# Block products of the pair stages gathered onto each other's PSUM banks, with ScalarE copying out in between

## The chip, the core and the metric

The kernel runs on one core of one Trainium2 chip. The metric is the device time of one launch in microseconds; the median of three runs is given. A core has five engines with a queue each: TensorE (PE in the rows, its weight loads PEld), VectorE (DVE), ScalarE (ACT), GpSimd (POOL) and SyncE (SP, which issues the DMAs). Each engine works its queue off in order and waits on semaphores for the others.

## The reference

Three stages follow each other: attention with a band mask, a mixture of four experts, and a gated network.

```python
scores = scale * np.matmul(q, k.transpose(0, 1, 3, 2)) + bias      # 2 x 8 heads, 768 positions, 64 wide
a = softmax(np.where(keep, scores, -1e9));  attn = a @ v           # keep: 8 global keys or 96 local ones
p = domain_probs / (domain_probs.sum(-1, keepdims=True) + 1e-09)   # x: 1536 tokens x 512
for e in range(4):
    out += p[:, e:e+1] * (np.maximum(x @ w1[e], 0.0) @ w2[e])      # 512 -> 1024 -> 512
h = (x @ w1) * (x @ w2)                                            # 512 -> 1024, twice
return (h @ w3) @ w_out                                            # 1024 -> 1024 -> 512
```

All of it is in float32. The last two weights are multiplied with each other first (w34 = w3 @ w_out).

## The kernel before

Every float32 operand of the large products is split into a high and a low half: `split` (L49, L50) casts the high half on ScalarE and subtracts it from the source on VectorE or GpSimd. The helper `three` (L55 to L57) then runs three matmuls of 128 x 128 by 128 x 512: high by high, high by low, low by high. Tokens stand in three chunks of 512 columns, 0 to 2.

Engines are written in program order (`manual_schedule`): what the code issues first on an engine runs first there.

**The pair stages.** For part of the work two chunks of tokens (1 and 2) and two row blocks of weights are taken together as a 2 by 2 block product, which needs seven block products in place of eight, on sums and differences of blocks. The blocks of the weights are a11, a12, a22 and the sums s1 to s4, those of the tokens b11 to b22 and the differences t1 to t4. One block product is `product(a, b)`: six matmuls onto one PSUM bank (`z`, four banks in turn). From the seven products the four results are added up:

c11 = a11 b11 + a12 b21; with u2 = a11 b11 + s2 t2, c12 = u2 + s1 t1 + s4 b22; with u3 = u2 + s3 t3, c22 = u3 + s1 t1 and c21 = u3 + a22 t4.

There are two such stages:

- The expert pair stage has eight steps (0 to 7): steps 0 to 3 for expert 3, steps 4 to 7 for expert 2, each for two of the eight hidden rows of that expert. `Pairs.run` does a step. Between the products it calls `issue(j)` (the down products onto the banks `o` that are due, twelve matmuls each; after the last of a row, four multiplications by the gate share on VectorE, L749, and four additions on GpSimd, L750), `prep(0)` (casts of the next step's weights a11, a12, a22), `prep(1)` (their four sums, L642, on VectorE, then casts and low halves on ScalarE and GpSimd) and, in steps 4 to 7, `prep(2)` (casts and low halves of two down weights of the second expert, on ScalarE and VectorE). `out` ends a result: ReLU to the high half on ScalarE (L541), low half on VectorE (L542).
- The gate pair stage has eight steps too. `Gate.run` does one: the same products; two of the four results are multiplied by the other two (L1124, L1128) and split. `issue(n)` there is three matmuls of the final product of the step before. `sums_of_w` (L1066) and the casts prepare the next step's weights.

Before, each of the seven products of a step goes to a bank of its own. ScalarE copies the first (L661, L1101), and VectorE adds the other six in seven additions (L649, L1097), two of them from s1's bank.

Of the kernel before, what the change touches and what calls it, by code (L numbers as in the profile page):

```python
# [8 lines left out]
F32 = mybir.dt.float32  # L9
# [4 lines left out]
ALU = mybir.AluOpType  # L14
# [4 lines left out]
P = 128  # L19
# [8 lines left out]
CW = 512  # L28
# [9 lines left out]
LAG = 2  # L38
# [14 lines left out]
def three(nc, out, wh, wl, xh, xl, start, stop):  # L53

    nc.tensor.matmul(out, wh, xh, start=start, stop=False)  # L55
    nc.tensor.matmul(out, wh, xl, start=False, stop=False)  # L56
    nc.tensor.matmul(out, wl, xh, start=False, stop=stop)  # L57
# [524 lines left out]
class Pairs:  # L582


# [62 lines left out]
    def run(self, n, issue, prep, out):  # L647
        nc, tmp = self.nc, self.tmp
        add = lambda o, a, b: nc.vector.tensor_tensor(o, a, b, op=ALU.add)  # L649

        def product(a, b):
            z = self.ps_z.tile([P, CW], F32, name="z")
            h, l = self.at(n, ("a11", "a12", "a22", "s1", "s2", "s3", "s4").index(a))
            xh, xl = self.x_operand(b)
            for k in range(2):
                ks = slice(k * P, (k + 1) * P)
                three(nc, z, h[:, ks], l[:, ks], xh[:, k], xl[:, k], k == 0, k == 1)
            return z

        s1, s6 = tmp(), tmp()  # L660
        nc.scalar.copy(s1, product("a11", "b11"))  # L661
        add(s6, s1, product("s2", "t2"))
        prep(0)
        issue(0)
        add(s1, s1, product("a12", "b21"))
        out(0, 1, s1)
        u3 = tmp()
        add(u3, s6, product("s3", "t3"))
        prep(1)
        issue(1)  # L670
        z = product("s1", "t1")
        c22 = tmp()
        add(c22, u3, z)
        add(s6, s6, z)
        out(1, 2, c22)
        prep(2)
        issue(2)
        add(u3, u3, product("a22", "t4"))
        out(1, 1, u3)
        issue(3)  # L680
        add(s6, s6, product("s4", "b22"))
        out(0, 2, s6)


def experts_and_gate(tc, g, x_hi, x_lo, slots, experts, first_time):

    nc = tc.nc
    name = "" if first_time else "g"
    with ExitStack() as ctx:
# [142 lines left out]
        for n in range(last + 1):  # L832
            i, gr = divmod(n, FC // 2)
            e = pairs[i]
            if gr:
                downs = [[(e, 1, 2 * gr - 2)], [], [(e, 1, 2 * gr - 1)], []]
            elif i:
                downs = ends(pairs[i - 1])
            else:
                downs = [work[-LAG:], [], [], []]  # L840
# [125 lines left out]
class Gate:  # L966
# [111 lines left out]
    def run(self, f, between):  # L1078
# [3 lines left out]

        def product(a, b):
            z = self.ps_z.tile([P, CW], F32, name="z")
            h, l = blocks[a]
            xh, xl = self.x_operand(b)
            for k in range(2):
                ks = slice(k * P, (k + 1) * P)
                three(nc, z, h[:, ks], l[:, ks], xh[:, k], xl[:, k], k == 0, k == 1)
            return z  # L1090

        def issue(n):
            if between[n]:
                between[n]()

        more = bool(self.fetched)
        add = lambda out, a, b: nc.vector.tensor_tensor(out, a, b, op=ALU.add)  # L1097
        part = (lambda n: self.sums_of_w(n)) if more else (lambda n: None)
        s1 = self.pool.tile([P, CW], F32, name="prob")
        s6, u3, c22, c11 = self.tmp  # L1100
        nc.scalar.copy(s1, product("a11", "b11"))  # L1101
        add(s6, s1, product("s2", "t2"))
        if more:
            self.split_w()
        issue(0)
        add(c11, s1, product("a12", "b21"))
        part(0)
        part(1)
        add(u3, s6, product("s3", "t3"))
# [5 lines left out]
        z = product("s1", "t1")  # L1115
        add(c22, u3, z)
        h2 = self.pool.tile([P, CW], F32, name="t", bufs=3)
        add(h2, s6, z)
        issue(2)
        z = product("a22", "t4")  # L1120
        hh, hl = self.place()
        h1 = self.pool.tile([P, CW], F32, name="t", bufs=3)
        add(h1, u3, z)
        nc.vector.tensor_tensor(h1, h1, c11, op=ALU.mult)  # L1124
        split(nc, hh, hl, h1)
        issue(3)
        add(h2, h2, product("s4", "b22"))
# [124 lines left out]
```

## Time and profile before

| | |
|---|---|
| median of three runs | 835.33 us (835.03 to 836.26) |
| span of the profiled execution (the time the profile gives for it) | 833.3 us |
| TensorE busy | 821.4 us, 4006 matmuls |
| VectorE, ScalarE, GpSimd busy | 518.4, 288.4, 310.1 us |
| expert pair stage, its eight steps | 427.4 to about 570 us |
| gate pair stage | 703.7 to 801.7 us |

The span runs from the first to the last instruction of the program in the trace; the device time of a run also holds what lies around it. Matmuls are pipelined: a matmul of 512 columns is shown with 0.39 us, though the next starts sooner, so starts are compared here, not durations. In a row of a timeline stand the start, the duration, the engine, the line, the operation, output and inputs, the shape and the count of merged operations; square brackets give the idle time ahead and what ended it.

### The profile page before, as it was taken

To read this page: it belongs to the slowest core of one execution; us is meant where nothing else is said; L and a number is where in the kernel's file an instruction comes from. 1 tells how busy PE (TensorE), PEld (TensorE's weight loads), DVE (VectorE), ACT (ScalarE), POOL (GpSimd) and SP (SyncE) were. 2 spreads that over 40 slices of the span, in tenths; PEclk is the share of its full clock that TensorE was granted. 3 is DMA by queue.
4 is the path that set the end of the run, shared out by engine and by line. 5 is a ranking of instruction groups with operands and counts; after the bars stand their busy time and mean duration, and the time that the engine had idled before them with its cause. 6 is when DMAs were issued, how large, how long until landed. Compare 5 with 4: busy or idle time off the path is not lost.

```text
span 833.3 us, 11131 instructions
## 1 busy us (share of the span) xinstructions
PE 821.4 (99%) x4006; PEld 668.4 (80%) x4006; DVE 518.4 (62%) x962; ACT 288.4 (35%) x609; POOL 310.1 (37%) x318
## 2 busy tenths in 40 slices
PE   8999999999999999999999999999999999999996
PEld 4777888888888888888888888888788888888875
DVE  7998355557755556787738563665633743887840
ACT  6998221223321213333314321332443332333210
POOL 3687013534356564560344341422380003333300
PEclk9999999999999999999999999999999999999999
DMA  6762233547553456643101101020522210201011
GB/s 217 228 202 78 77 115 113 160 154 232 175 165 113 160 170 192 214 162 114 63 26 52 39 25 64 35 81 25 190 99 86 93 53 26 101 26 52 1 51 55
DMA packets 38709, 89.22 MB, mean 107 GB/s; under 512 B 3896, under 2 KB 10344, under 8 KB 38644
## 3 DMA queue, kind: packets, MB, share of 16 engines
q1 hardware_dynamic: 38644, 88.41, 32.7%
q8 instruction: 34, 0.56, 0.3%
q14 instruction: 31, 0.25, 0.1%
HBM read 74.74 MB, written 13.66 MB: 106 GB/s over the span
## 4 chain that ended last, share of the span: by engine, by line
PE 89%; POOL 3%; ACT 3%; DVE 2%; issue 1%; DMA 0%; SPq 0%; POOLq 0%; ACTq 0%; DVEq 0%
PE z L55 18%; PE z L57 18%; PE z L56 18%; PE o L57 11%; PE o L55 11%; PE o L56 11%; POOL pt L308 2%; ACT pt L269 2%; POOL sl L50 1%; DVE t L262 1%; ACT ptT L294 0%; DMA words<-in_n_local_dram 0%; PE sp L55 0%; PE sp L56 0%; PE sp L57 0%
## 5 line engine op out<-in xcount | busy, mean ns | idle before, releaser
L57 PE MATMUL z<-xh,sl 128*128 128x512 f32 x428 | 166.5, 389 | 0.0
L55 PE MATMUL z<-xh,sh 128*128 128x512 f32 x428 | 166.5, 389 | 0.0
L56 PE MATMUL z<-xl,sh 128*128 128x512 f32 x428 | 166.5, 389 | 0.0
L498 POOL TENSOR_TENSOR cr<-cr,cb 128x512 f32<-128x512 f32 x40 | 51.6, 1289 | 125.3 <-issue 118.8
L50 POOL TENSOR_TENSOR sl<-wr,sh 128x256 fp32r<-128x256 f32 (+1 forms) x44 | 40.8, 943 | 150.0 <-ACT sh L49 149.7
L57 PEld LDWEIGHTS z<-xh,sl 128*128 128x128 f32 x428 | 80.4, 188 | 17.2 <-DVE sl L50 0.2
L55 PEld LDWEIGHTS z<-xh,sh 128*128 128x128 f32 x428 | 80.4, 188 | 16.5
L56 PEld LDWEIGHTS z<-xl,sh 128*128 128x128 f32 x428 | 80.3, 188 | 16.6
L50 DVE TENSOR_TENSOR sl<-wr,sh 128x1024 fp32r<-128x1024 f32 (+1 forms) x57 | 70.7, 1245 | 23.1 <-ACT sh L49 22.4
L49 ACT CAST sh<-wr 128x1024 fp32r<-128x1024 f32 (+2 forms) x101 | 75.4, 766 | 21.3 <-PE z L56 10.3
L750 POOL TENSOR_TENSOR acc<-acc,t 128x512 f32<-128x512 f32 x36 | 49.3, 1404 | 84.8 <-DVE t L749 84.8
L483 POOL TENSOR_SCALAR ca<-ca 128x512 f32<-128x512 f32 x40 | 61.5, 1537 | 36.8 <-DMA raw<-in_w_out_dram 36.8
L649 DVE TENSOR_TENSOR t<-t,z 128x512 f32<-128x512 f32 x56 | 37.4, 680 | 32.0 <-PE z L57 27.7
L55 PE MATMUL z<-sh,sh 128*128 128x512 f32 x128 | 49.9, 390 | 0.8 <-DVE t L749 0.8
L56 PE MATMUL z<-sl,sh 128*128 128x512 f32 x128 | 49.8, 389 | 0.0
L57 PE MATMUL z<-sh,sl 128*128 128x512 f32 x128 | 49.8, 389 | 0.0
L269 ACT ACTIVATE pt<-t,negmax 128x256 f32<-128x256 f32 (+1 forms) x96 | 45.9, 479 | 8.9 <-DVE negmax L262 7.7
L308 POOL TENSOR_TENSOR pt<-pt,r 128x256 f32<-128x256 f32 (+1 forms) x72 | 40.8, 595 | 15.3 <-DVE r L237 12.6
L262 DVE CUSTOM_DVE_ANT_0 t<-sp,bias 128x256 f32<-128x256 f32 (+1 forms) x96 | 34.6, 393 | 1.8 <-ACT bias L224 0.4
L50 POOL TENSOR_TENSOR sl<-t,sh 128x256 fp32r<-128x256 f32 (+1 forms) x24 | 23.0, 973 | 31.3 <-ACT sh L49 31.0
L55 PE MATMUL o<-h0h,sh 128*128 128x512 f32 x84 | 32.8, 390 | 0.0
L57 PE MATMUL o<-h0h,sl 128*128 128x512 f32 x84 | 32.7, 389 | 0.0
(254 smaller groups left out, 1738.9 us busy)
## 6 DMA issues: line engine op xcount, KB each, us to landing
wr<-in_w_moe_dram SPq DMA_DIRECT2D x44, 512.0 KB, 4.4
raw<-in_w3t_dram SPq DMA_DIRECT2D x16, 512.0 KB, 4.3
raw<-in_w_ab_dram SPq DMA_DIRECT2D x16, 512.0 KB, 4.6
wr<-wab_d SPq DMA_DIRECT2D x16, 512.0 KB, 3.3
raw<-in_w_out_dram SPq DMA_DIRECT2D x8, 512.0 KB, 5.0
w3t_d<-cr SPq DMA_DIRECT2D x16, 256.0 KB, 2.5
wab_d<-cr SPq DMA_DIRECT2D x16, 256.0 KB, 2.4
wr<-w3t_d SPq DMA_DIRECT2D x8, 512.0 KB, 3.3
```

Source lines behind the costliest of these rows:

```text
L49: nc.scalar.copy(hi, src)
L50: (lo_engine or nc.vector).tensor_tensor(lo, src, hi.bitcast(F32), op=ALU.subtract)
L55: nc.tensor.matmul(out, wh, xh, start=start, stop=False)
L56: nc.tensor.matmul(out, wh, xl, start=False, stop=False)
L57: nc.tensor.matmul(out, wl, xh, start=False, stop=stop)
L262: nc.vector.tensor_tensor_reduce(out=t[:, 0:w], in0=sp[hh % 2][:, hh // 2, 0:w], in1=bb, scale=-SCALE, scalar=3.0e38, op0=ALU.add, op1=ALU ...
L269: nc.scalar.activation(pt[:, hh, 0:w], t[:, 0:w], AF.Exp, bias=g.negmax[:, u * H + h : u * H + h + 1], scale=-1.0, accum_out=sums[:, h : h ...
L308: nc.gpsimd.tensor_tensor(pt[:, hh, 0:w], pt[:, hh, 0:w], r[:, hh : hh + 1].to_broadcast([P, w]), op=ALU.mult)
L483: nc.gpsimd.tensor_scalar(a, a, 2.0**-15, None, op0=ALU.max)
L498: nc.gpsimd.tensor_tensor(rest, rest, top.bitcast(F32), op=ALU.add)
L649: add = lambda o, a, b: nc.vector.tensor_tensor(o, a, b, op=ALU.add)
L750: nc.gpsimd.tensor_tensor(acc[c][:, d], acc[c][:, d], t, op=ALU.add)
```

## The change

The products of a step that belong to one sum are added up in PSUM: `product(a, b, onto)` runs its six matmuls onto a bank that holds an earlier product. Two banks are used so: `first` holds a11 b11, then also s2 t2 (u2), then s3 t3 (u3), then a22 t4 (c21); `both` holds s1 t1 and then also s4 b22. Between, ScalarE copies what is needed on its own: p1 = a11 b11, u2 and u3. VectorE keeps three additions: c11 = p1 + a12's bank, c22 = u3 + `both`, c12 = u2 + `both`. c21 is read from `first` itself. The products are issued in the order a11, a12, s2, s1, s3, a22, s4. In the expert stage the downs of steps 0 to 3 and 5 to 7 are issued after s2 and after s3, `prep(1)` after c22's `out`, and `prep(2)` after a22's `out`. `skip_group_check` is a flag of the program's builder.

```diff
--- before.py
+++ after.py
@@ -50,11 +50,11 @@
     (lo_engine or nc.vector).tensor_tensor(lo, src, hi.bitcast(F32), op=ALU.subtract)
 
 
-def three(nc, out, wh, wl, xh, xl, start, stop):
-
-    nc.tensor.matmul(out, wh, xh, start=start, stop=False)
-    nc.tensor.matmul(out, wh, xl, start=False, stop=False)
-    nc.tensor.matmul(out, wl, xh, start=False, stop=stop)
+def three(nc, out, wh, wl, xh, xl, start, stop, more=False):
+
+    nc.tensor.matmul(out, wh, xh, start=start, stop=False, skip_group_check=more)
+    nc.tensor.matmul(out, wh, xl, start=False, stop=False, skip_group_check=more)
+    nc.tensor.matmul(out, wl, xh, start=False, stop=stop, skip_group_check=more)
 
 
 def iota_f32(nc, pool, width, base, step, name):
@@ -581,6 +581,7 @@
 
 class Pairs:
 
+    BLOCKS = ("a11", "a12", "a22", "s1", "s2", "s3", "s4")
 
 
     def __init__(self, nc, pool, tmp, ps_z, experts):
@@ -646,40 +647,57 @@
 
     def run(self, n, issue, prep, out):
         nc, tmp = self.nc, self.tmp
-        add = lambda o, a, b: nc.vector.tensor_tensor(o, a, b, op=ALU.add)
-
-        def product(a, b):
-            z = self.ps_z.tile([P, CW], F32, name="z")
-            h, l = self.at(n, ("a11", "a12", "a22", "s1", "s2", "s3", "s4").index(a))
-            xh, xl = self.x_operand(b)
-            for k in range(2):
-                ks = slice(k * P, (k + 1) * P)
-                three(nc, z, h[:, ks], l[:, ks], xh[:, k], xl[:, k], k == 0, k == 1)
-            return z
-
-        s1, s6 = tmp(), tmp()
-        nc.scalar.copy(s1, product("a11", "b11"))
-        add(s6, s1, product("s2", "t2"))
+        product = Products(nc, self.ps_z, self.x_operand, lambda a: self.at(n, self.BLOCKS.index(a)))
+
+        first = product("a11", "b11")
+        p1 = product.copy(first, tmp())
+        z = product("a12", "b21")
+        c11 = product.plus(z, p1, tmp())
+        product("s2", "t2", first)
+        u2 = product.copy(first, tmp())
         prep(0)
         issue(0)
-        add(s1, s1, product("a12", "b21"))
-        out(0, 1, s1)
-        u3 = tmp()
-        add(u3, s6, product("s3", "t3"))
+        out(0, 1, c11)
+        both = product("s1", "t1")
+        product("s3", "t3", first)
+        u3 = product.copy(first, tmp())
+        issue(1)
+        c22 = product.plus(both, u3, tmp())
+        out(1, 2, c22)
         prep(1)
-        issue(1)
-        z = product("s1", "t1")
-        c22 = tmp()
-        add(c22, u3, z)
-        add(s6, s6, z)
-        out(1, 2, c22)
+        product("a22", "t4", first)
+        out(1, 1, first)
         prep(2)
         issue(2)
-        add(u3, u3, product("a22", "t4"))
-        out(1, 1, u3)
+        product("s4", "b22", both)
+        out(0, 2, product.plus(both, u2, tmp()))
         issue(3)
-        add(s6, s6, product("s4", "b22"))
-        out(0, 2, s6)
+
+
+class Products:
+
+
+    def __init__(self, nc, ps_z, x_operand, w_operand):
+        self.nc, self.ps_z, self.x, self.w = nc, ps_z, x_operand, w_operand
+
+    def __call__(self, a, b, onto=None):
+
+        more = onto is not None
+        z = onto if more else self.ps_z.tile([P, CW], F32, name="z")
+        h, l = self.w(a)
+        xh, xl = self.x(b)
+        for k in range(2):
+            ks = slice(k * P, (k + 1) * P)
+            three(self.nc, z, h[:, ks], l[:, ks], xh[:, k], xl[:, k], k == 0 and not more, k == 1, more)
+        return z
+
+    def copy(self, z, to):
+        self.nc.scalar.copy(to, z)
+        return to
+
+    def plus(self, z, more, to):
+        self.nc.vector.tensor_tensor(to, more, z, op=ALU.add)
+        return to
 
 
 def experts_and_gate(tc, g, x_hi, x_lo, slots, experts, first_time):
@@ -833,11 +851,11 @@
             i, gr = divmod(n, FC // 2)
             e = pairs[i]
             if gr:
-                downs = [[(e, 1, 2 * gr - 2)], [], [(e, 1, 2 * gr - 1)], []]
+                downs = [[(e, 1, 2 * gr - 2)], [(e, 1, 2 * gr - 1)], [], []]
             elif i:
                 downs = ends(pairs[i - 1])
             else:
-                downs = [work[-LAG:], [], [], []]
+                downs = [[w] for w in work[-LAG:]] + [[], []]
 
             def issue(j):
                 for e, c, f in downs[j]:
@@ -1079,52 +1097,44 @@
 
         nc = self.nc
         blocks = self.made.pop(0)
-
-        def product(a, b):
-            z = self.ps_z.tile([P, CW], F32, name="z")
-            h, l = blocks[a]
-            xh, xl = self.x_operand(b)
-            for k in range(2):
-                ks = slice(k * P, (k + 1) * P)
-                three(nc, z, h[:, ks], l[:, ks], xh[:, k], xl[:, k], k == 0, k == 1)
-            return z
+        product = Products(nc, self.ps_z, self.x_operand, blocks.__getitem__)
 
         def issue(n):
             if between[n]:
                 between[n]()
 
         more = bool(self.fetched)
-        add = lambda out, a, b: nc.vector.tensor_tensor(out, a, b, op=ALU.add)
         part = (lambda n: self.sums_of_w(n)) if more else (lambda n: None)
-        s1 = self.pool.tile([P, CW], F32, name="prob")
-        s6, u3, c22, c11 = self.tmp
-        nc.scalar.copy(s1, product("a11", "b11"))
-        add(s6, s1, product("s2", "t2"))
+        u2, u3, c22, c11 = self.tmp
+        first = product("a11", "b11")
+        p1 = product.copy(first, self.pool.tile([P, CW], F32, name="prob"))
+        z = product("a12", "b21")
+        product.plus(z, p1, c11)
+        product("s2", "t2", first)
+        product.copy(first, u2)
         if more:
             self.split_w()
-        issue(0)
-        add(c11, s1, product("a12", "b21"))
         part(0)
         part(1)
-        add(u3, s6, product("s3", "t3"))
+        both = product("s1", "t1")
+        issue(0)
+        product("s3", "t3", first)
+        product.copy(first, u3)
         part(2)
         part(3)
         if more:
             self.split_s()
         issue(1)
-        z = product("s1", "t1")
-        add(c22, u3, z)
-        h2 = self.pool.tile([P, CW], F32, name="t", bufs=3)
-        add(h2, s6, z)
         issue(2)
-        z = product("a22", "t4")
+        product.plus(both, u3, c22)
+        product("a22", "t4", first)
         hh, hl = self.place()
         h1 = self.pool.tile([P, CW], F32, name="t", bufs=3)
-        add(h1, u3, z)
-        nc.vector.tensor_tensor(h1, h1, c11, op=ALU.mult)
+        nc.vector.tensor_tensor(h1, c11, first, op=ALU.mult)
         split(nc, hh, hl, h1)
         issue(3)
-        add(h2, h2, product("s4", "b22"))
+        product("s4", "b22", both)
+        h2 = product.plus(both, u2, self.pool.tile([P, CW], F32, name="t", bufs=3))
         nc.vector.tensor_tensor(h2, h2, c22, op=ALU.mult)
         split(nc, *self.waiting[f], h2)
         return hh, hl
```

The next rows are VectorE's in step 0 of the expert pair stage, before the change: L749 the multiplications after a down, L649 the additions, L542 low halves, L642 the sums of weights.

```order
L649 TENSOR_TENSOR t<-t,z 128x512
L749 TENSOR_TENSOR t<-o_4047,prob 128x512
L749 TENSOR_TENSOR t<-o_4048,prob 128x512
L749 TENSOR_TENSOR t<-o_4049,prob 128x512
L749 TENSOR_TENSOR t<-o_4050,prob 128x512
L649 TENSOR_TENSOR t<-t,z 128x512
L542 SCALAR_TENSOR_TENSOR h0l<-t,h0h 128x512
L649 TENSOR_TENSOR t<-t,z 128x512
L642 TENSOR_TENSOR t<-wr 128x256
L642 TENSOR_TENSOR t<-t,wr 128x256
L642 TENSOR_TENSOR t<-wr 128x256
L642 TENSOR_TENSOR t<-wr,t 128x256
```

And the same place after the change (the additions are now L699, the multiplications L767, the sums L643).

```order
L699 TENSOR_TENSOR t<-t,z 128x512
L542 SCALAR_TENSOR_TENSOR h0l<-t,h0h 128x512
L767 TENSOR_TENSOR t<-o_4047,prob 128x512
L767 TENSOR_TENSOR t<-o_4048,prob 128x512
L767 TENSOR_TENSOR t<-o_4049,prob 128x512
L767 TENSOR_TENSOR t<-o_4050,prob 128x512
L699 TENSOR_TENSOR t<-t,z 128x512
L542 SCALAR_TENSOR_TENSOR xl_74<-t,xh_71 128x512
L643 TENSOR_TENSOR t<-wr 128x256
L643 TENSOR_TENSOR t<-t,wr 128x256
L643 TENSOR_TENSOR t<-wr 128x256
L643 TENSOR_TENSOR t<-wr,t 128x256
```

The four multiplications stood behind the first of the step's additions and stand now behind c11's low half and ahead of c22's addition, with the weight sums behind that; seven additions have become three.

Next ScalarE around the end of step 5, before the change: L49 casts, of weights (`wr`) and of their sums (`t`), L541 the ReLUs, L661 the copy of the next step's first product.

```order
L49 CAST sh_83<-t 128x256
L541 ACTIVATE xh_71<-t 128x512
L49 CAST sh_81<-wr 128x512
L49 CAST sh_83<-wr 128x512
L541 ACTIVATE h1h<-t 128x512
L541 ACTIVATE xh_71<-t 128x512
L661 COPY t<-z 128x512
```

And after it (the copies are L695).

```order
L49 CAST sh_83<-t 128x256
L541 ACTIVATE h1h<-z 128x512
L49 CAST sh_81<-wr 128x512
L49 CAST sh_83<-wr 128x512
L541 ACTIVATE xh_71<-t 128x512
L695 COPY t<-z 128x512 x2
```

The ReLU of c21 now reads the bank (`z`); it and the copy after c12's ReLU have the casts of the sums and of the down weights ahead of them, as the copy had before.

Last TensorE at the start of a step of the gate pair stage, before the change, with what each waits for: six matmuls of a11 (`xh_72,sh_1560`; the last three stand here) and the first of s2 (`sh_83,sh_1562`).

```order
L55 MATMUL z<-xh_72,sh_1560 128x512
L56 MATMUL z<-xl_75,sh_1560 128x512
L57 MATMUL z<-xh_72,sl_1561 128x512
L55 MATMUL z<-sh_83,sh_1562 128x512 [waits DVE_49,Activation_49]
L56 MATMUL z<-sl_84,sh_1562 128x512
L57 MATMUL z<-sh_83,sl_1563 128x512 [waits Pool_49]
L55 MATMUL z<-sh_83,sh_1562 128x512
```

And after it.

```order
L55 MATMUL z<-xh_72,sh_1560 128x512
L56 MATMUL z<-xl_75,sh_1560 128x512
L57 MATMUL z<-xh_72,sl_1561 128x512
L55 MATMUL z<-xh_72,sh_1560 128x512
L56 MATMUL z<-xl_75,sh_1560 128x512
L57 MATMUL z<-xh_72,sl_1561 128x512
L55 MATMUL z<-xh_72,sh_1560 128x512
L56 MATMUL z<-xl_75,sh_1560 128x512
L57 MATMUL z<-xh_72,sl_1561 128x512
L55 MATMUL z<-sh_83,sh_1562 128x512 [waits Activation_49]
```

a12's six matmuls stand between now, and s2's first matmul, which goes onto a11's bank, waits for ScalarE alone.

## Rows read from the trace of the kernel before

**Rows 1.** The page, part 1: busy us, share of the span, instructions.
```profile
PE 821.4 (99%) x4006; PEld 668.4 (80%) x4006; DVE 518.4 (62%) x962; ACT 288.4 (35%) x609; POOL 310.1 (37%) x318
```

**Rows 2.** Table of stretches: length, busy of each engine, granted clock, DMA.
```profile
427.40:570.00 142.60, 142.32 (x628) 117.58 (x627) 87.49 (x134) 43.48 (x82) 49.25 (x47) 1.00 0.14 46
703.70:801.70 98.00, 98.00 (x433) 80.92 (x431) 75.70 (x114) 28.66 (x53) 34.11 (x30) 1.00 0.12 38
```

**Rows 3.** Timeline of TensorE at the end of step 0: start, duration, operation.
```profile
443.51 0.39 PE L57 MATMUL z<-xh,sl 128*128 128x512 f32 x1
444.17 0.47 PE L55 MATMUL z<-t2h,sh 128*128 128x512 f32 x1 [0.28 <-ACT xh L541]
444.48 0.39 PE L56 MATMUL z<-t2l,sh 128*128 128x512 f32 x1
```

**Rows 4.** Timeline of TensorE at the end of the gate pair stage.
```profile
799.39 0.39 PE L57 MATMUL z<-sh,sl 128*128 128x512 f32 x1
...
801.43 0.39 PE L57 MATMUL z<-xh,sl 128*128 128x512 f32 x1
801.93 0.50 PE L55 MATMUL o<-w34h,h2h 128*128 128x512 f32 x1
802.27 0.39 PE L56 MATMUL o<-w34l,h2h 128*128 128x512 f32 x1
...
803.00 0.40 PE L55 MATMUL o<-w34h,h2h 128*128 128x512 f32 x1
```

**Rows 5.** Timeline of VectorE there.
```profile
799.81 0.69 DVE L1097 TENSOR_TENSOR t<-acc,z 128x512 f32<-128x512 f32 x1 [0.76 <-PE z L57]
800.53 0.69 DVE L1124 TENSOR_TENSOR t<-t,acc 128x512 f32<-128x512 f32 x1
801.91 0.69 DVE L50 TENSOR_TENSOR h2l<-t,h2h 128x512 fp32r<-128x512 f32 x1 [0.69 <-ACT h2h L49]
```

**Rows 6.** Timeline of ScalarE there.
```profile
801.26 0.62 ACT L49 CAST h2h<-t 128x512 fp32r<-128x512 f32 x1 [8.43 <-DVE t L1124]
```

**Rows 7.** Timeline of VectorE at the end of step 5.
```profile
532.92 0.69 DVE L542 SCALAR_TENSOR_TENSOR h3l<-t,h3h 128x512 fp32r<-128x512 f32 x1 [0.70 <-ACT h3h L541]
...
534.13 0.42 DVE L642 TENSOR_TENSOR t<-wr 128x256 f32<-128x256 f32 x1
534.65 0.42 DVE L642 TENSOR_TENSOR t<-t,wr 128x256 f32<-128x256 f32 x1
...
535.33 0.96 DVE L642 TENSOR_TENSOR t<-wr,t 128x256 f32<-128x256 f32 x1
...
538.68 1.28 DVE L50 TENSOR_TENSOR sl<-wr,sh 128x512 fp32r<-128x512 f32 x2
```

**Rows 8.** Timeline of ScalarE there.
```profile
536.33 0.41 ACT L49 CAST sh<-t 128x256 fp32r<-128x256 f32 x1 [0.26 <-DVE t L642]
...
537.46 1.12 ACT L49 CAST sh<-wr 128x512 fp32r<-128x512 f32 x2
...
542.58 0.63 ACT L541 ACTIVATE xh<-t 128x512 fp32r<-128x512 f32 x1 [1.36 <-DVE t L649]
543.12 0.57 ACT L661 COPY t<-z 128x512 f32<-128x512 f32 x1
```

**Rows 9.** Timeline of GpSimd there.
```profile
535.06 0.95 POOL L50 TENSOR_TENSOR sl<-t,sh 128x256 fp32r<-128x256 f32 x1 [5.52 <-ACT sh L49]
```

**Rows 10.** Timeline of VectorE in step 0.
```profile
433.73 2.80 DVE L749 TENSOR_TENSOR t<-o,prob 128x512 f32<-128x512 f32 x4 [2.64 <-PE o L57]
...
438.58 1.57 DVE L542 SCALAR_TENSOR_TENSOR h0l<-t,h0h 128x512 fp32r<-128x512 f32 x1 [0.76 <-ACT h0h L541]
```

**Rows 11.** Timeline of GpSimd in step 0.
```profile
434.57 5.03 POOL L750 TENSOR_TENSOR acc<-acc,t 128x512 f32<-128x512 f32 x4 [2.42 <-DVE t L749]
```

**Rows 12.** Line 542 from PSUM: durations in ns (least, median, most), first and last start.
```profile
L542 DVE SCALAR_TENSOR_TENSOR h3l<-z,h3h x16: 683/692/694, 99.0 to 425.6; 128x512 fp32r<-128x512 f32 x16
```

**Rows 13.** Table of stretches: the last 13 us, columns as in rows 2.
```profile
820.00:833.00 13.00, 7.02 (x31) 5.47 (x30) 1.12 (x2) 0.37 (x1) 0.00 (x0) 0.91 0.14 48
```

## The prediction

> **What bounds the kernel now.** I read the page's part 1 first: TensorE is busy for 821.4 of 833.3 us [rows 1]. So only its 11.9 us of idle time can be won, and any new wait of TensorE is paid in full. Next the table of stretches: in the expert pair stage (427.4 to 570.0) TensorE is busy for 142.32 of 142.60 us, in the gate pair stage (703.7 to 801.7) for 98.00 of 98.00 [rows 2]. Then TensorE's timeline, for the places where a matmul does not start one pitch after the one before. The pitch is 0.227 us: nine matmuls from 799.39 to 801.43 [rows 4]. In the two stages I find two gaps. At 443.51 the next two starts come after 0.66 and 0.31 us [rows 3], 0.52 us over two pitches. At 801.43 four starts take 1.57 us [rows 4], 0.66 over. If the change took away both and added nothing, the time would fall by 1.2 us.
>
> How late releases are paid is in the second gap: the cast that TensorE waits for ends at 801.26+0.62 = 801.88 [rows 6], the matmul starts at 801.93 and the next 0.34 later, 0.11 over the pitch [rows 4]. So a release that ends at E moves the stream as if the matmul had started at E+0.16.
>
> **The change part by part.** The matmuls stay the same in number and size, so TensorE's work is unchanged; the flag in `three` adds no instruction. VectorE drops four of seven additions a step, ScalarE gains two copies. Neither engine is the bound, so this is worth nothing by itself; what counts is who waits.
>
> *What is new on TensorE's path.* Before, each product had a bank of its own, and s2's product (the third of a step now) could start whatever ScalarE did. Now it adds onto the bank of a11's product, and must wait until ScalarE has copied p1 out of it. Behind it stands TensorE's whole queue. That copy is ScalarE's first work of a step, behind the last cast or ReLU of the step before, which waits for VectorE's addition to s4's product. So each step's end must run through VectorE and ScalarE within two products. I follow this chain for each kind of boundary, from hand-offs as the trace has them: a matmul's start to VectorE 0.42 (799.39 to 799.81 [rows 4, 5]; I take the same for ScalarE), engine to engine 0.03 to 0.04, and the next operation of an engine 0.09 before the reported end of the one ahead (542.58+0.63 against 543.12 [rows 8]).
>
> *Ordinary expert boundary (steps 1-2, 2-3, 3-4).* Zero is the start of s3's last matmul. The copy of u3 runs 0.42 to 0.99 (0.57 [rows 8]); c22's addition to 1.71 (0.69, as at 799.81 [rows 5]); its ReLU 1.74 to 2.37 (0.63 [rows 8]); its low half 2.40 to 3.09 (0.69 [rows 7]). The four sums of the next weights follow at 3.00: second 0.52 later, fourth 0.68 after that [rows 7], at 4.20. The fourth is held by GpSimd: GpSimd starts 0.93 after the first sum (534.13 to 535.06 [rows 7, 9]), runs 0.95, and the sum ends 0.28 after it (535.33+0.96 [rows 7]): 5.16. The last weight cast follows to 5.61 (0.41 [rows 8]). Only then comes the ReLU of a22's bank, though a22's last matmul started 18 pitches after zero, at 4.08: in the new order it stands behind those casts. It runs 5.52 to 6.15, its low half 6.18 to 6.87 (0.69 for that operation from PSUM, 683 to 694 ns in all of them [rows 12]), c12's addition 6.78 to 7.47, its ReLU to 8.13, p1's copy 8.04 to 8.61. The matmul is due 37 pitches after zero, at 8.39, and goes as if at 8.77: 0.38 late. Three times: +1.1. Bounds: 0.16 each without the reload (0.3 to +0.5 in all), 0.7 each if GpSimd also holds a second operation.
>
> On that last point the trace shows VectorE's low half of two SBUF tensors taking 1.57 us while GpSimd adds [rows 10, 11] and 0.69 from PSUM [rows 12]. GPSIMD Engine Reference of the Trainium skill, section 1 (Specifications), says that the two share SBUF interfaces and contend when VectorE has two SBUF inputs. By that rule the low half of a22's bank, read from PSUM, is not held, and the sum stays; were it held, 0.4 would be added three times.
>
> *Boundaries with down weights (5-6, 6-7).* Here two casts and two subtractions of the second expert's weights now stand between a22's ReLU and c12's addition; before they stood ahead of a22's addition, and nothing on TensorE waited. The casts run 6.06 to 7.18 (1.12 [rows 8]); the subtractions 6.78 to 8.06 (1.28 for two [rows 7]). c12's addition then runs 7.97 to 8.66, ReLU to 9.32, copy 9.23 to 9.80, as if at 9.96: 1.57 late. Twice: +3.2 (2.6 without reload; 4.0 with GpSimd in the way). After step 7 TensorE goes on with downs whose third matmul needs the first subtraction. No sums stand ahead here: a22's ReLU 4.50 to 5.13, casts from 5.04, low half to 5.85, subtraction 5.76 to 6.44, matmul due 27 pitches after zero, 6.13: +0.5 (0.2 to 0.6).
>
> *Step 0 to 1.* Its second down is the last of its row and is moved from before a12 to after s3, and with it four multiplications of 2.80 us in all [rows 10], which stand ahead of c22's addition. The first can start 0.42 after the down's third matmul, at 1.10; they end at 3.90. c22 then runs 3.81 to 4.50, its ReLU to 5.16. GpSimd adds from 0.84 after the first multiplication (433.73 to 434.57) for 5.03 us [rows 10, 11], to 6.97. The low half of c22, two SBUF tensors, meets that: in the trace it ended 0.55 after GpSimd (438.58+1.57 = 440.15 against 439.60). So it ends at 7.52, the sums start at 7.43 in place of 3.00, and the rest of the chain comes 4.43 later: 0.38+4.43 = 4.8 late. The 0.52 of rows 3, which stood at the same boundary, is swallowed: net +4.3. Lower bound, with no contention: sums at 5.79, net +2.65. I take 4.3, the nearest row being of the same kind.
>
> *Step 4* has 24 to 36 matmuls of downs after s3, a22 and s4, so nothing is late: 0.
>
> *Gate boundaries (seven).* Zero is the start of a22's last matmul. VectorE's product with c11 starts at 0.42 (the addition ahead of it is gone); cast 0.73 after it, subtraction 0.65 after that (800.53, 801.26, 801.91 [rows 5, 6]): 1.15 and 1.80. s4's last matmul is nine later, at 2.04, so its addition starts at 2.46, the product 0.72 later at 3.18, the cast at 3.91, p1's copy 0.53 later, 4.44 to 5.01. Due are 22 pitches, 4.99; as if at 5.17: 0.18 late. Seven times: +1.3 (0 to +2.1). At the last step the missing addition brings the cast 0.72 earlier, and the gap of rows 4 goes: -0.66.
>
> Sum: 4.3 + 1.1 + 3.2 + 0.5 + 1.3 - 0.7 = +9.7 us on the profiled 833.3, 843.0. The profile gives that execution's span alone; the median of the runs, 835.33, lies 2.0 above it, which I take for what lies around the span. So 845.0.
>
> **The rivals.**
> A, the forecast: the chains hold: 845, by the bounds 840.5 to 848.
> B, only part holds: VectorE's operations slip between GpSimd's additions at step 0 and the down weights run early enough. Then 2.65 + 0.5 + 1.5 + 0.2 + 0.6 - 0.7 = +4.8: 840. For it: GpSimd is idle in much of both stages (49.25 of 142.6 us busy [rows 2]); against it: rows 10 show the wait at just that place.
> C, the other side: p1's copy is always in time, because ScalarE is idle for two thirds of the stages [rows 2]; it would need each chain to be some 0.4 us shorter in the gate, and 1.6 or more where weights stand in it. Then both gaps go: 834.1, within 0.2% (1.7 us, about what a measurement here can tell from no change).
> D, the clock falls: at step 0 TensorE would stand still for some 4 us. The trace shows the granted clock at 0.91 over the last 13 us [rows 13], where its work ends at 827, and at 1.00 in both stages, where its gaps are under 1 us. At the lower of the two levels (1.2 for 2.4 GHz) each pitch doubles: 3 to 4 us of matmuls after that wait at half speed cost 3 to 4 us more: 849. That TensorE's clock is taken down after an idle window is also what the Trainium skill says in TensorE: Matmul & The Clock Gate, part 1.
>
> **How the numbers follow.** A 0.68, B 0.13, D 0.09, C 0.10. The likeliest gives 845.0. The range leaves out C and a little of D: 839 to 849. Faster by over 0.2% would need more than the two gaps hold: 0.01. Same: C, 0.09. Slower: 0.90.
>
> **What would show it.** In the profile after: waits of TensorE at the product line for ScalarE's copy, once a step: one near 4.8 us at the first expert boundary, two near 1.6, three near 0.4, seven near 0.2 in the gate, and no gap before the last finals. TensorE's busy time stays near 821; VectorE's falls by some 40 us (64 additions of 0.68). If these waits are under 1 us in sum, I am wrong about ScalarE's order; if they are much longer, about contention or the clock.

## The result and the profile after

The changed kernel takes 847.94 us (847.29 to 848.93, four runs), the kernel before 835.18 beside it: a ratio of 1.0149, 95% interval 1.0135 to 1.0163. It is 12.8 us slower, where 9.7 were forecast: 845.0 was 2.9 us too low, inside the range. Some executions of most kernels here take about 1.5 us longer and, where one of them was profiled, lose it in the first 20 us, ahead of all that the change touches; so what an edit does is read from gaps in the trace first, and from the medians second.

The page's part 1 of the kernel after, which answers to [rows 1]:

```profile
PE 826.9 (98%) x4006; PEld 668.5 (79%) x4006; DVE 469.7 (56%) x898; ACT 303.9 (36%) x641; POOL 313.0 (37%) x318
```

VectorE lost 48.7 us and 64 instructions, none of it to TensorE's profit: TensorE has the same 4006 matmuls and is busy 5.5 us longer, though its work is the same. Part of it must be slower work, or waits too short to show as idle time. The waits of TensorE in the kernel after (engine, line waited for: us in total, times, longest):

```profile
PE z L55 <- ACT t L695: 7.8, 6, 4.0
...
PE z L55 <- DVE t L767: 0.7, 1, 0.7
```

The first row is new: six waits for ScalarE's copies. The second, at the first matmul behind the last down, was there before (0.8). The first row leaves out the seven of the gate, which are too short to show as idle time. TensorE at the boundary of steps 0 and 1, after:

```profile
445.25 0.39 PE L57 MATMUL z<-xh,sl 128*128 128x512 f32 x1
449.63 0.79 PE L55 MATMUL z<-t2h,sh 128*128 128x512 f32 x1 [4.00 <-ACT t L695]
450.23 0.63 PE L56 MATMUL z<-t2l,sh 128*128 128x512 f32 x1
450.65 0.63 PE L57 MATMUL z<-t2h,sl 128*128 128x512 f32 x1
...
452.79 0.47 PE L56 MATMUL o<-h0l,sh 128*128 128x512 f32 x1
```

This is [rows 3] after the change. Behind a wait of 4.0 us the starts come 0.43 apart, not 0.227, up to 452.79. The table of stretches shows the granted clock beside them (columns as in [rows 2]):

```profile
449.60:452.70 3.10, 3.06 (x7) 2.48 (x8) 0.83 (x2) 0.05 (x1) 0.00 (x0) 0.50 0.03 5
551.20:555.00 3.80, 3.72 (x16) 3.09 (x17) 0.88 (x2) 1.97 (x5) 0.73 (x1) 1.00 0.54 181
```

The granted clock is 0.50 there, the lower of its two levels, and 1.00 behind the wait of 1.58 us at 549. The chain ahead of the wait of 4.0 us runs through VectorE, with GpSimd beside it:

```profile
437.90 2.68 DVE L767 TENSOR_TENSOR t<-o,prob 128x512 f32<-128x512 f32 x4 [3.10 <-PE o L57]
440.49 0.68 DVE L699 TENSOR_TENSOR t<-t,z 128x512 f32<-128x512 f32 x1
441.87 1.16 DVE L542 SCALAR_TENSOR_TENSOR xl<-t,xh 128x512 fp32r<-128x512 f32 x1 [0.70 <-ACT xh L541]
442.95 1.50 DVE L643 TENSOR_TENSOR t<-wr 128x256 f32<-128x256 f32 x1
```

```profile
438.67 5.50 POOL L768 TENSOR_TENSOR acc<-acc,t 128x512 f32<-128x512 f32 x4 [3.27 <-DVE t L767]
```

As predicted, the multiplications stand ahead of c22's addition, and GpSimd's additions (to 444.17) hold the low half (1.16 against 0.69) and the first sum (1.50 against 0.42). The late addition also delays TensorE directly: s4's product in step 0 goes onto the bank `both`, which c22's addition reads until 440.49 + 0.68 = 441.17.

```profile
440.82 0.39 PE L57 MATMUL z<-t4h,sl 128*128 128x512 f32 x1
441.22 0.50 PE L55 MATMUL z<-xh,sh 128*128 128x512 f32 x1
441.56 0.40 PE L56 MATMUL z<-xl,sh 128*128 128x512 f32 x1
```

That is 0.29 us over two pitches, too short to show as idle time. The other waits in the expert stage, one of each kind:

```profile
466.03 0.39 PE L57 MATMUL z<-xh,sl 128*128 128x512 f32 x1
466.79 0.50 PE L55 MATMUL z<-t2h,sh 128*128 128x512 f32 x1 [0.37 <-ACT t L695]
467.12 0.39 PE L56 MATMUL z<-t2l,sh 128*128 128x512 f32 x1
...
549.31 0.39 PE L57 MATMUL z<-xh,sl 128*128 128x512 f32 x1
551.28 0.50 PE L55 MATMUL z<-t2h,sh 128*128 128x512 f32 x1 [1.58 <-ACT t L695]
```

And a boundary in the gate, where no idle time is shown and only the starts tell (0.32 and 0.34 in place of two pitches):

```profile
729.84 0.39 PE L57 MATMUL z<-xh,sl 128*128 128x512 f32 x1
730.16 0.50 PE L55 MATMUL z<-sh,sh 128*128 128x512 f32 x1
730.50 0.39 PE L56 MATMUL z<-sl,sh 128*128 128x512 f32 x1
```

The gap of [rows 4] before the last finals is gone. TensorE's last matmul starts 12.3 us later than before (838.93 against 826.63), and the lowest runs lie as far apart (847.29 and 834.96).

### The profile page after: what moved, and what is told of

Its sections match the earlier page's. It is cut to its first block, busy times and chain, and to the rows that moved or that the text cites. A ratio compares the mean times of both kernels' runs of the same rounds, so it can differ in the third digit from the quotient of the medians.

```text
span 845.5 us, 11067 instructions
## 1 busy us (share of the span) xinstructions
PE 826.9 (98%) x4006; PEld 668.5 (79%) x4006; DVE 469.7 (56%) x898; ACT 303.9 (36%) x641; POOL 313.0 (37%) x318
## 4 chain that ended last, share of the span: by engine, by line
PE 83%; DVE 5%; ACT 5%; POOL 3%; issue 2%; DMA 0%; SPq 0%; ACTq 0%; POOLq 0%; DVEq 0%
PE z L55 17%; PE z L57 16%; PE z L56 16%; PE o L57 11%; PE o L55 11%; PE o L56 11%; ACT pt L269 2%; POOL pt L308 2%; DVE t L643 2%; DVE t L699 1%; POOL sl L50 1%; ACT t L695 1%; DVE sl L50 0%; ACT ptT L294 0%; DMA words<-in_n_local_dram 0%
## 5 line engine op out<-in xcount | busy, mean ns | idle before, releaser
L50 POOL TENSOR_TENSOR sl<-wr,sh 128x256 fp32r<-128x256 f32 (+1 forms) x44 | 43.3, 1000 | 164.8 <-ACT sh L49 164.5
L49 ACT CAST sh<-wr 128x1024 fp32r<-128x1024 f32 (+2 forms) x101 | 75.5, 768 | 21.4 <-PE z L56 10.3
L695 ACT COPY t<-z 128x512 f32<-128x512 f32 x24 | 14.0, 582 | 56.1 <-PE z L57 56.1
L699 DVE TENSOR_TENSOR t<-t,z 128x512 f32<-128x512 f32 x24 | 16.4, 682 | 31.9 <-ACT t L695 21.4
```

The lines of the kernel that those rows point to most:

```text
L49: nc.scalar.copy(hi, src)
L50: (lo_engine or nc.vector).tensor_tensor(lo, src, hi.bitcast(F32), op=ALU.subtract)
L699: self.nc.vector.tensor_tensor(to, more, z, op=ALU.add)
```

## The experiments

Theory: the gathered banks make TensorE wait for a chain that runs through ScalarE and VectorE at each step's end, and each boundary's lateness is set by what is queued ahead of p1's copy. Rivals: the chain's own length, or the clock, or the accumulation itself.

**Step 0's down moved back** (e1).

```diff
-                downs = [[w] for w in work[-LAG:]] + [[], []]
+                downs = [work[-LAG:], [], [], []]
```

> Only the second of step 0's two down products goes back to its place of before (both ahead of s1's product); everything else is as in the changed kernel (847.9 us). Theory: TensorE's 4.0 us wait at the boundary of steps 0 and 1 comes from the four multiplications of that down (2.80 us on VectorE) and GpSimd's four additions (5.03 us), which stand ahead of c22's addition and of its low half; and the seven slow starts behind the wait (0.427 us in place of 0.227) come from the wait. Without both the boundary should be an ordinary one, 0.4 to 0.9 us late in place of 6.1: 842.3 us, 841.5 to 843.0. Rival 1: the wait comes from the order of the sums and casts alone, as at the other boundaries, and is longer there for a reason of the first step (GpSimd's load of another kind): then the time stays within 1 us of 847.9. Rival 2: the slow starts are not a result of the wait: then only 4.0 to 4.4 us go, 843.6, and slow starts are still seen after 445 us.

Measured: 846.03 us, ratio to before 1.0131 (1.0115 to 1.0146): a gain of 5.6 us expected, under 2 seen. TensorE:

```profile
439.46 0.39 PE L57 MATMUL z<-t3h,sl 128*128 128x512 f32 x1
440.57 0.50 PE L55 MATMUL z<-t4h,sh 128*128 128x512 f32 x1 [0.73 <-ACT t L695]
...
445.94 0.39 PE L57 MATMUL z<-xh,sl 128*128 128x512 f32 x1
448.24 0.50 PE L55 MATMUL z<-t2h,sh 128*128 128x512 f32 x1 [1.91 <-ACT t L695]
```

My expectation had forgotten what the down covers. Its twelve matmuls stood between s3 and a22; without them a22, which adds onto the bank whose copy u3 has only begun, waits at once, and only 25 pitches (5.68 us) lie between s3's last matmul and the late one, not 37 (8.39). The chain itself did become ordinary: from 439.46 to the copy's end at 448.19 are 8.73 us, at the boundary of steps 1 and 2 of the changed kernel 8.9. But 8.73 + 0.16 - 5.68 is 3.2 late, and the clock fell again (0.58 over 448.2 to 452.0). The miss is no evidence against the multiplications; it needed an edit that leaves the cover.

**Only the multiplications late** (e6), the down left in its place:

```diff
...
                 for e, c, f in downs[j]:
+                    if n == 0 and j == 1:
+                        state["hold"] = True      # down() then leaves its multiplications out
                     down(e, c, f, order.get(c))
+                if n == 0 and j == 3:
+                    finish(*state.pop("held"))    # the multiplications and GpSimd's additions
```

> Only the four multiplications of step 0's second down, and GpSimd's four additions that follow them, are issued later: behind c12's result in place of right behind the down. The down's matmuls stay where they are behind s3, so that, other than in the run that moved the whole down back, the 12 matmuls still stand between c22 and the late copy. Theory: the 4.0 us wait is the multiplications' and GpSimd's; without them this boundary is like the other three (0.43 to 0.64 late) and the clock stays: 6.3 + 0.3 - 0.6 = 5.7 to 6.0 us go: 842.1 us, 841.5 to 843.0. Rival: the sums and casts of the weights hold the chain at this boundary whatever stands before them, as the run with the down moved back, still 4.8 us late, may be read: 845 to 848 us. Second rival: TensorE then waits for the o banks at step 1's first down, since the multiplications read them last: a new wait of 1 to 3 us, 843 to 845.

Measured: 841.85 us, 1.0076 (1.0064 to 1.0088), as the theory said. Neither rival's time or wait is seen.

```profile
444.80 0.39 PE L57 MATMUL z<-xh,sl 128*128 128x512 f32 x1
445.35 0.50 PE L55 MATMUL z<-t2h,sh 128*128 128x512 f32 x1 [0.16 <-ACT t L695]
445.68 0.40 PE L56 MATMUL z<-t2l,sh 128*128 128x512 f32 x1
```

The boundary is 0.43 late like the others, with the pitch of the full clock behind it, and s4's product of step 0 is in time.

**GpSimd's additions left out** (e7), the multiplications kept in place.

```diff
...
-                    nc.gpsimd.tensor_tensor(acc[c][:, d], acc[c][:, d], t, op=ALU.add)
+                    if not state.get("no_adds"):      # set for step 0's second down
+                        nc.gpsimd.tensor_tensor(acc[c][:, d], acc[c][:, d], t, op=ALU.add)
```

> Left out: GpSimd's four additions of the second down of step 0 to the running sum of the experts (the multiplications stay, their products are used no further). Theory: these additions hold VectorE's low half of c22 (1.16 in place of 0.69 us) and the first weight sum (1.50 in place of 0.42), together 1.55 us of the 4.0; the wait falls to some 2.4 us. If the clock still falls after it, the time is 1.6 lower, 846.3 us; if it stays, 3.2 lower, 844.7. Rival: GpSimd is not what holds them (the wait stays at 4.0 and the time at 847.9), for instance because GpSimd's low halves of the weights, which are still there, hold as much.

Measured: 845.57 us (844.34 to 845.9). VectorE and TensorE:

```profile
441.87 0.69 DVE L542 SCALAR_TENSOR_TENSOR xl<-t,xh 128x512 fp32r<-128x512 f32 x1 [0.70 <-ACT xh L541]
442.48 0.42 DVE L643 TENSOR_TENSOR t<-wr 128x256 f32<-128x256 f32 x1
```

```profile
448.02 0.50 PE L55 MATMUL z<-t2h,sh 128*128 128x512 f32 x1 [2.38 <-ACT t L695]
448.36 0.39 PE L56 MATMUL z<-t2l,sh 128*128 128x512 f32 x1
448.59 0.40 PE L57 MATMUL z<-t2h,sl 128*128 128x512 f32 x1
448.82 0.41 PE L55 MATMUL z<-t2h,sh 128*128 128x512 f32 x1
449.05 0.61 PE L56 MATMUL z<-t2l,sh 128*128 128x512 f32 x1
```

The two held operations are back at 0.69 and 0.42 and the wait falls from 4.00 to 2.38: GpSimd's share is 1.62, the prediction's difference between its two bounds (1.65). In this execution the clock still fell, only a microsecond after the wait (0.51 over 449.0 to 452.5). Two of the five runs, at 844.3 and 844.6, are where the time would be without that fall, and their granted clock is 0.998 on the mean, 0.996 in the other three, which fits; but only the profiled run has a trace, so where in those two the clock stayed is not shown.

**The wait filled with work** (e5).

```diff
+        again = 3 if n == 1 else 0
...
         z = product("a12", "b21")
+        for _ in range(again):
+            product("a12", "b21", z, again=True)      # starts the bank afresh
...
```

> Work added: in step 1 of the expert stage a12's product is run three more times onto its own bank, each time starting the bank afresh, so the values stay the same: 18 matmuls, 18 x 0.227 = 4.09 us, that stand just where TensorE waits 4.0 us for p1's copy. Theory: the wait is filled by them, and the slow starts behind it (0.43 in place of 0.23 us, seven of them, 1.6 us) were the granted clock's answer to the idle wait: they go, and the time falls by 1.6 although TensorE does more: 846.3 us, 845.9 to 846.7. Rival: the slow starts belong to the work itself there (both operands just written, or contention with GpSimd and VectorE): 847.9 with the slow starts still to be seen. Second rival: the extra matmuls hold the release of a12's bank and so c11 and all behind it: over 849 us.

Measured: 847.04 us (845.87 to 848.85), 0.7 over the expected 846.3 and outside its range. The profiled run is 1.7 us late already ahead of the edit's place (s4's product of step 0 starts at 442.88, in the changed kernel at 441.22), so the stage itself is what tells:

```profile
450.99 0.39 PE L57 MATMUL z<-xh,sl 128*128 128x512 f32 x1
451.31 0.50 PE L55 MATMUL z<-t2h,sh 128*128 128x512 f32 x1
451.65 0.39 PE L56 MATMUL z<-t2l,sh 128*128 128x512 f32 x1
```

```profile
449.60:452.70 3.10, 3.10 (x14) 2.29 (x13) 1.88 (x3) 1.11 (x2) 0.11 (x1) 1.00 0.41 154
```

With 18 more matmuls the clock stays at 1.00 and the slow starts are gone: they were the answer to the idle wait. The late start that is left, at 451.31, is an ordinary one of 0.20. That TensorE's clock is taken down after idleness is what the Trainium skill says in TensorE: Matmul & The Clock Gate, part 1; these two runs agree (0.50 with the wait, 1.00 with it filled). The lowest run is 1.4 below the lowest of the changed kernel (847.29), for 1.6 expected.

**The weight sums early** (e2).

```diff
         out(0, 1, c11)
+        prep(1)
...
         out(1, 2, c22)
-        prep(1)
```

> Only the four sums of the next step's weights, their casts and their low halves are issued earlier: behind c11's result in place of behind c22's. Theory: at each boundary it is these, by way of GpSimd's hold on the fourth sum, that make a22's ReLU, c12's addition and p1's copy late. Ordinary boundaries should then not be late (1.56 us go), those with down weights by about 0.55 each in place of 1.8 (2.5 us go), that of steps 0 and 1 by some 1.6 us without the slow starts behind it (4.5 us go): about 839.4 us, 837.5 to 841.5. Rival: the lateness is that of the chain of c22, a22, c12 and the copy itself (its length on ScalarE and VectorE, whatever else is queued): then the time stays at 846 to 848 us. Second rival: the sums do the same harm earlier, by holding c22's addition behind GpSimd: then waits of TensorE appear at s4's product, and 843 to 848 us.

Measured: 838.13 us, 1.0032 (1.002 to 1.0043): 9.8 us go by the medians, 9.2 by the start of the last matmul (829.69 against 838.93), for 8.5 expected. TensorE's waits for the copies shrink to one row:

```profile
PE z L55 <- ACT t L695: 0.8, 3, 0.3
```

The three are steps 0 to 1 (0.54 late, for 1.6 expected) and the two with down weights (0.54 each). At the first, the multiplications and GpSimd's additions are where they were, so most of their harm came by way of the sums and casts queued behind c22. The first rival does not hold: the same additions, ReLUs and copies run, and the three ordinary boundaries are in time. Of the second a little is left: s4's product of step 0 waits for c22's addition as in the changed kernel, 0.38 us in place of 0.29.

```profile
440.75 0.39 PE L57 MATMUL z<-t4h,sl 128*128 128x512 f32 x1
441.25 0.50 PE L55 MATMUL z<-xh,sh 128*128 128x512 f32 x1
```

**The down weights early** (e3) and **the gate's final product first** (e4).

```diff
         out(0, 1, c11)
+        prep(3)      # steps 5 to 7: the down weights, before in prep(2) behind a22's out
...
```

> Only the casts and subtractions of the second expert's down weights in steps 5 to 7 are issued earlier: behind c11's result in place of behind a22's. Theory: at the boundaries of steps 5-6 and 6-7 (1.85 and 1.75 us late in the changed kernel) they are what is late beyond the 0.5 us of an ordinary boundary, and after step 7 their subtraction is the whole 0.47: 2.5 + 0.4 = 2.9 us go, 845.0 us, 844.3 to 845.8. Rival: their place does not matter, since VectorE and ScalarE have the same work in a step either way and the sums hold the chain (GpSimd): then 847 to 848 us with the two waits still above 1.2 us. Second rival: earlier in the step they hold c11's or c22's chain and the slots of the weights they replace are still read: new waits, over 848 us.

Measured: 844.22 us, 1.0109 (1.0094 to 1.0125).

```profile
549.21 0.39 PE L57 MATMUL z<-xh,sl 128*128 128x512 f32 x1
549.78 0.50 PE L55 MATMUL z<-t2h,sh 128*128 128x512 f32 x1 [0.18 <-ACT t L696]
```

The two boundaries are 0.46 and 0.37 late instead of 1.85 and 1.75, and the 0.47 after step 7 is gone: 3.2 by the trace, for 2.9 expected.

```diff
         product.plus(z, p1, c11)
+        issue(0)
         product("s2", "t2", first)
...
-        issue(0)
         product("s3", "t3", first)
```

> Only in the gate pair stage: the three matmuls of the final product that stood behind s1's product are issued between a12's and s2's product, so that the matmul which waits for p1's copy is due three pitches (0.68 us) later. Theory: the seven gate boundaries are late by 0.2 each because the copy ends 5.0 us after the step's last but one product and the matmul is due then; with 0.68 more in hand all seven waits go: -1.4 us, 846.5 us, 846.2 to 846.8. Rival: what looks like a wait for the copy is the change of the accumulation bank itself (a matmul that adds onto an older bank costs 0.2 us wherever it stands): then 847.9, and the gaps of 0.2 stay at s2's product with ScalarE's copy long done.

Measured: 846.67 us, 1.0135 (1.012 to 1.0151). In the gate every start is one pitch after the last:

```profile
730.74 0.39 PE L57 MATMUL o<-w34h,h0l 128*128 128x512 f32 x1
730.96 0.39 PE L55 MATMUL z<-sh,sh 128*128 128x512 f32 x1
```

All seven gaps are gone, so the bank's change costs nothing here and lateness was all.

**All four together** (e8: e2, e3, e4, e6), **then step 1's sums behind u3's copy** (e9).

> Four edits together: the weight sums early, the down weights of steps 5 to 7 early, the gate's final product ahead of s2, and step 0's multiplications late. Theory: what the run with the sums early alone left (838.1 us) goes too: 0.9 at steps 0 to 1, 1.1 at the boundaries 5-6 and 6-7, 0.5 after step 7, 1.3 to 1.4 in the gate: 838.1 - 3.9 = 834.2 us, 833.8 to 834.9, against 835.3 for the kernel before, which has two gaps of 0.5 and 0.7 that are gone here. Rival: with all the waits for p1's copy gone the next late release shows (c22's ReLU behind the early casts, or c11's low half behind the down weights): 835.3 to 838 us, no gain over the kernel before.

Measured: 835.07 us, 0.9997 (0.9988 to 1.0005), just over the expected range. The rival was right in part: one new wait for a copy, this time u3's.

```profile
455.88 0.39 PE L57 MATMUL o<-h1h,sl 128*128 128x512 f32 x1
456.76 0.50 PE L55 MATMUL z<-t4h,sh 128*128 128x512 f32 x1 [0.49 <-ACT t L696]
```

```diff
-                if j == 1 and n < last:
+                if j == (4 if n == 1 else 1) and n < last:
...
         issue(1)
+        prep(4)
```

> The four edits together as before, and in step 1 alone the weight sums stand behind the copy of u3. Theory: the one gap that the four edits left in the expert stage (0.66 us at 455.88 and 0.11 behind it, a22's product of step 1 waiting for the copy of u3) comes from GpSimd's four additions, now late, which hold the early sums of step 1 (1.50, 1.33, 0.95 and 0.96 us in place of 0.42) and with them the casts ahead of that copy. With the copy ahead of the casts the gap goes: 834.2 us against 835.0. Rival: the gap moves on to c12's addition or to the next p1 copy: 834.7 to 835.4.

Measured: 834.02 us, 0.9983 (0.9974 to 0.9992); the gap is gone (a22's product starts at 454.62, a pitch behind 454.39) and went nowhere else.

**One edit outside the change**, on top of e9 (e10) and on the kernel before (e11):

```diff
-            for s in (f,) if c == 2 and f != 7 else ():
+            for s in {5: (), 6: (5, 6), 7: ()}.get(f, (f,)) if c == 2 else ():
```

> The same, and one edit that has nothing to do with the change: at the end of the experts one subtraction of 1.23 us of the gate's weights is issued behind the last row's multiplications in place of ahead of them. Theory: the gap of 0.9 to 1.0 us at the first matmul behind the last down (596.39 in the kernel before, 598.34 with the four edits) is the wait for the first of those multiplications, which stands behind that subtraction: 833.2 us, faster than the kernel before by 0.2%. Rival: another wait (the slot whose subtraction is late) takes its place: 834.2.

> The kernel before with only that last edit (a subtraction of 1.23 us behind the last row's multiplications). Theory: its gap of 1.03 us goes likewise: 834.3 us. So the best version of the gathered products would stand about 1.1 us below the best of the separate ones (the two gaps of 0.52 and 0.66), and no more, because VectorE's spared time is off the path. Rival: 835.3, no change.

Measured: 833.05 us, 0.9973 (0.9962 to 0.9984), and 834.09 us, 0.9984 (0.9975 to 0.9993). In e10 the gap behind the last down is a pitch (597.31 to 597.54). So e10 is 0.3% below the kernel before, but 1.2 us of that are an old gap that the kernel before could lose too. Between the best versions of both schemes lie 1.0 us, the two gaps that the prediction named (0.52 and 0.66). That is all that gathering the products brought here. Whether the kernel before could lose those two gaps as well, by moving its own side work, no run tested.

## Why the prediction was right, point by point

| step | predicted | measured in the trace |
|---|---|---|
| steps 0 to 1, lateness, net of [rows 3] | +4.3 | +4.3 (0.3 of it at s4's product) |
| the same, lower clock behind it | 0 (rival D: 3 to 4) | +1.5 |
| ordinary boundaries, three | +1.1 | +1.6 (0.64, 0.43, 0.49) |
| with down weights, two | +3.2 | +3.6 (1.85, 1.75) |
| after step 7 | +0.5 | +0.5 |
| gate, seven | +1.3 | +1.4 |
| end of the gate | -0.7 | -0.7 |
| sum | +9.7 | +12.2, of 12.3 at the last matmul |

The measured numbers are starts over the pitch of 0.227. The rest is pitches of 0.23 to 0.24 behind late starts, some 0.3 in sum, less 0.13 by which the old gap behind the last down got shorter. The mechanism held at every late copy of the expert stage: TensorE waits for p1's copy, which stands behind c12's ReLU; that waits for c12's addition, which stands behind a22's low half and so behind all that is queued ahead of a22's ReLU. In the gate the copy stands behind the cast of the step's last product, as forecast. The prediction counted the first boundary from s3's last matmul, so the wait of s4's product is inside its 4.8; by its own times it should have named it (c22's addition ends at 4.50, s4's product is due 19 pitches after zero, at 4.31). Three terms were mis-sized.

*The clock.* "Step 0 to 1" left out the half-rate matmuls. What came is rival D, A with a fall of the clock behind it, which the prediction gave 0.09; only its price was smaller. The 3 to 4 us of matmuls at half speed come from no row; the runs showed seven or eight starts and 1.5 to 1.7 us. So the likeliest case was not quite the one that came, and the time fell into the range because D cost about half of what was put down for it. A wait of that length should have stood in the forecast with at least part of that price, since [rows 13] showed a fall and no row showed such a wait without one.

*The hand-off to ScalarE.* I took a matmul's start to ScalarE as 0.42, like VectorE's. In the trace after it is 0.48 to 0.50, at step 1 even 0.76. This, with copies of 0.59 in place of 0.57, is about the excess of the ordinary boundaries: at step 1 s3's last matmul starts at 457.87 and the copy of u3 at

```profile
458.63 0.59 ACT L695 COPY t<-z 128x512 f32<-128x512 f32 x1 [4.03 <-PE z L57]
```

*The down weights.* Their two subtractions took 1.48, not 1.28 [rows 7], the case that the prediction gave as a bound (GpSimd in the way):

```profile
547.41 0.69 DVE L542 SCALAR_TENSOR_TENSOR h1l<-z,h1h 128x512 fp32r<-128x512 f32 x1 [0.97 <-ACT h1h L541]
548.01 1.48 DVE L50 TENSOR_TENSOR sl<-wr,sh 128x512 fp32r<-128x512 f32 x2
```

```profile
546.35 1.99 POOL L50 TENSOR_TENSOR sl<-t,sh 128x512 fp32r<-128x512 f32 x2 [0.20 <-ACT sh L49]
```

GpSimd works until 548.34; the subtraction, with two SBUF inputs, starts at 548.01 and is held, while the low half read from PSUM, at 547.41, takes its usual 0.69 beside GpSimd. So the choice to hold the one and not the other was right for the low half and one subtraction short. By the rule in GPSIMD Engine Reference of the Trainium skill, section 1 (Specifications), it would come out so.

Rival B fell at step 0 (the additions did hold), C at every boundary but step 4's, where the prediction expected no wait and none came. VectorE lost 48.7 us, not some 40: 64 additions of 0.68 are 43.5. The last weight sum of the gate's steps (L1066 before, L1084 after, `sums<-wr,sums`, eight times) also became shorter, 1.38 us on the mean before and 0.42 after, 7.7 in all, which is more than the other 5; what stood against it was not followed.

## What to carry to other kernels

To add a product onto a bank that must be copied out first turns a free bank into a chain: price it as time from the last producer to the copy's end against the matmuls in between, queue by queue, and count what every moved block covers as well as what it holds up. When the bound engine is at 99%, work saved elsewhere is worth only the gaps it closes (1.0 us here), and each new wait is paid in full, with the clock on top if it falls, as it did behind the wait of 4.0 us here. Before dropping such a scheme, move the side work (sums, casts, multiplications) ahead of the chain: that took 847.9 to 834.0.

## What the hardware showed that was not expected

- The clock fell behind waits of 4.00, 2.38 and 1.91 us (the last with one of 0.73 some 6 us before), not behind 1.58. At 2.38 the first four matmuls still ran at the full rate. Seven or eight starts came about 0.43 apart, then the full pitch was back; the cost was 1.5 to 1.7 us each time.
- A matmul that goes late shows 0.47 to 0.50 in place of 0.39 and the next starts 0.08 to 0.11 over the pitch, also in the gate, where no idle time is shown: 0.09 late by the start alone, 0.20 in all. TensorE's weight loads, in the kernel after, suggest why: a load starts about a pitch ahead of its matmul (465.81 for the one at 466.03), but that of the late matmul starts with it, and the next load 0.10 behind. The prediction's bounds "without the reload" use a word that it does not explain; this may be what it means. No run tested it.

```profile
465.81 0.19 PEld L57 LDWEIGHTS z<-xh,sl 128*128 128x128 f32 x1
466.79 0.19 PEld L55 LDWEIGHTS z<-t2h,sh 128*128 128x128 f32 x1 [0.79 <-ACT t L695]
466.89 0.19 PEld L56 LDWEIGHTS z<-t2l,sh 128*128 128x128 f32 x1
```
